# A decode attention kernel: the ring of K and V tiles aligned, dealt out by order of release, with a constant lead of K over V

## The chip, the core and the metric

The kernel runs on one core of a Trainium2 chip. TensorE (PE) multiplies matrices into PSUM and loads its weights through PEld; VectorE (DVE), ScalarE (ACT) and GpSimd (POOL) work on elements; SyncE (SP) here does nothing but issue DMA transfers, in its program's order: a transfer that has to wait for its buffer holds up every later one on SP. All engines run their own instruction lists in order and wait for one another through semaphores. 16 DMA engines move the data; a 128-partition load is shared among them, eight rows each. The metric is the device time of the program in microseconds (us), lower is better: the median of several executions.

## What is computed

One token's attention over a long cache, and a small feed-forward network beside it, mixed by a gate:

```
q = (x @ wq) as 32 heads of 128           # x: 1 x 512
scores = q . K[h] * 128**-0.5             # K: 32 heads x 65536 x 128, bf16
p = softmax(scores);  o[h] = p @ V[h]     # V like K
a = concat(o) @ wo                        # 4096 x 512
b = (silu(x @ w_gate) * (x @ w_up)) @ w_down
g = sigmoid(sum(x * gate_w));  out = g * a + (1 - g) * b
```

K and V are 512 MiB each and are read once; there is one query, so almost no arithmetic is done on each byte.

## The kernel before

**Tiles.** A head's 65536 keys lie over the partitions as 128 rows of 512 keys. CUTS = (0, 172, 344, 512) makes three tiles of each head: 172, 172 and 168 keys a partition, that is rows of 44032 or 43008 bytes, 5504 or 5376 KB a tile. There are N = 96 K tiles and 96 V tiles, n = 3h + 0, 1, 2. A ring of four slots of 44032 bytes a partition holds everything large: wq, K and V tiles, the feed-forward weights (gu_t) and at the end half of wo. The ring is a pool with four buffers used in turn: each allocation takes the slot of the allocation four earlier, and the load into it waits until that slot's last reader is done.

**Work on a K tile** (`products`, `scores`). VectorE multiplies the tile by the head's query, broadcast over the keys (L230), and folds 128 products to 16 by three halving additions (L234). TensorE sums the last 16 with an identity matrix, 16 matmuls into the head's scores in PSUM (L245). This frees the K slot.

**Softmax of a head**, once its three K tiles are scored, in the step of the next head's first K tile: `row_max` takes the maximum (L257) and spreads it over the partitions with ScalarE and a matmul (L259, L261); `exponentials` makes the probabilities (L266 to L270). VectorE does them between a first part (64 keys) of that K tile's product and the rest. `total` and `weight` sum and invert (L279 to L285).

**Work on a V tile** (`values`, L294). TensorE takes four keys of each partition at a time, 43 or 42 matmuls of 128x4 weights against 128x512, into a 4x512 accumulator. This frees the V slot. After a head's third V tile `head_copy` copies the accumulator out (ScalarE), `head_row` brings its four blocks to one row of 128 scaled by gate and softmax sum, `turn` turns four heads' rows into columns of oT with four small matmuls, and `project` multiplies them with four blocks of wo into the result a_ps. wo's first half is loaded in four pieces on the way into a pool of its own (wo_sb); its second half at the end into a ring slot (wo_t).

**Order.** It is written out by hand: `steps` (L351 to L360) is a list of pairs (n, v), and the loop from L366 emits for each step, in this order: load of V tile v, load of K tile n (both on SP); head_row of a finished head; products of K tile n on VectorE, with the softmax of the previous head within them when n starts a head; `values(v)`, then `scores(n)` on TensorE. V starts at step 3 and is therefore three tiles behind K; at steps 23, 47 and 71 (SKIPS) no V tile is taken, so that V falls four, five and six tiles behind. At step 95 two V tiles are taken, and five more steps have V alone. The last two V tiles are loaded in pieces (V_CUTS), so that TensorE can start on them early. `feed_forward_in`, `feed_forward_mid` and `feed_forward_out` lie in steps 1 and 2.

At the end (L424 to L432): copy and row of head 31, the projections of the groups that were put off (`late`), the turn of the last group, the last projection, a cast and the output.

Of the kernel before, what the change touches and what calls it, by code (L numbers as in the profile page):

```python
# [8 lines left out]
ACT = mybir.ActivationFunctionType  # L9
ALU = mybir.AluOpType  # L10
AXIS = mybir.AxisListType
P = 128
# [4 lines left out]
SLOT = 172  # L17
SLOTS = 4

WIDTH = 16  # L20

SKIPS = (23, 47, 71)


@with_exitstack
def kernel(
# [14 lines left out]
    nc = tc.nc  # L41
# [10 lines left out]
    N = H * G  # L52
# [2 lines left out]
    assert all((b - a) % 4 == 0 and b - a <= SLOT for a, b in zip(CUTS[:-1], CUTS[1:]))  # L55
    scale = float(Dh) ** -0.5

    consts = ctx.enter_context(tc.tile_pool(name="consts", bufs=1))
    ring = ctx.enter_context(tc.tile_pool(name="ring", bufs=SLOTS))
    small = ctx.enter_context(tc.tile_pool(name="small", bufs=2))  # L60
    ppool = ctx.enter_context(tc.tile_pool(name="ppool", bufs=3))
    wo_pool = ctx.enter_context(tc.tile_pool(name="wo_pool", bufs=2))
    psum_s = ctx.enter_context(tc.tile_pool(name="psum_s", bufs=2, space=bass.MemoryType.PSUM))
    psum_o = ctx.enter_context(tc.tile_pool(name="psum_o", bufs=2, space=bass.MemoryType.PSUM))
    psum_a = ctx.enter_context(tc.tile_pool(name="psum_a", bufs=1, space=bass.MemoryType.PSUM))
# [1 line left out]

    ctx.enter_context(tc.manual_schedule())

    def big(name):  # L70
        return ring.tile([P, SLOT * Dh], bf16, name=name, tag="big")


    xT = consts.tile([P, KT], bf16, name="xT")
    gwT = consts.tile([P, KT], bf16, name="gwT")
    with nc.allow_non_contiguous_dma(reason="small"):
        nc.scalar.dma_start(out=xT, in_=A_x[0, 0, :].rearrange("(p t) -> p t", t=KT))
    wq_t = big("wq_t")
    wq_sb = wq_t[:, : KT * H * Dh].rearrange("p (t f) -> p t f", t=KT)
    nc.sync.dma_start(out=wq_sb, in_=A_wq.rearrange("(p t) f -> p t f", t=KT))  # L80

# [23 lines left out]
    def span(n):  # L105
        return CUTS[n % G], CUTS[n % G + 1]

    def load(dst, cache, n, name, cuts=None):
        h = n // G
        a, b = span(n)  # L110
        t = big(name)
        view = t[:, : (b - a) * Dh].rearrange("p (j d) -> p j d", d=Dh)
        src = cache[0, h, :, :].rearrange("(p j) d -> p j d", p=P)
        cuts = cuts or (0, b - a)
        for c, d in zip(cuts[:-1], cuts[1:]):
            nc.sync.dma_start(out=view[:, c:d, :], in_=src[:, a + c : a + d, :])
        dst[n] = view
# [17 lines left out]

    for g in range(H // QG):
        queries(g)


    gu_t = big("gu_t")  # L140
    wgu_sb = gu_t[:, : 2 * KT * F].rearrange("p (w t f) -> p w t f", w=2, t=KT)
    nc.sync.dma_start(out=wgu_sb[:, 0], in_=B_w_gate.rearrange("(p t) f -> p t f", t=KT))
    nc.sync.dma_start(out=wgu_sb[:, 1], in_=B_w_up.rearrange("(p t) f -> p t f", t=KT))
# [6 lines left out]

    WH = H // 2

    def load_wo_end(cuts):
        t = big("wo_t")[:, : (H - WH) * D].rearrange("p (g t n) -> p g t n", t=WG, n=D)
        rows = A_wo[WH * P :, :].rearrange("(g p t) n -> p g t n", p=P, t=WG)
        for a, b in zip(cuts[:-1], cuts[1:]):
            nc.sync.dma_start(out=t[:, a:b], in_=rows[:, a:b])
        for g in range((H - WH) // WG):
            wo_tiles[WH // WG + g] = t[:, g]

    def load_wo(g):
        wo_tiles[g] = wo_pool.tile([P, WG, D], bf16, name="wo_sb")
# [76 lines left out]
    def scores(n):  # L239
        h = n // G  # L240
        a, b = span(n)
        if a == 0:
            S_tiles[h] = psum_s.tile([P, NBH], f32, name="S_ps")
        for c in range(WIDTH):
            nc.tensor.matmul(  # L245
                S_tiles[h][:, a:b],
                lhsT=ident_b,
                rhs=K_tiles[n][:, :, c],
                start=(c == 0),
                stop=(c == WIDTH - 1),  # L250
            )
        del K_tiles[n]

    def row_max(h):

# [31 lines left out]
    def values(n):  # L287

        h = n // G
        a, b = span(n)  # L290
        if a == 0:
            O_tiles[h] = psum_o.tile([4, 4 * Dh], f32, name="O_ps")
        for j in range(a, b, 4):
            nc.tensor.matmul(  # L294
                O_tiles[h],
                lhsT=P_tiles[h][:, j : j + 4],
                rhs=V_tiles[n][:, j - a : j - a + 4, :],
                start=(j == 0),
                stop=(j == NBH - 4),
            )  # L300
        del V_tiles[n]

    def head_copy(h, last=False):
        O_sb = small.tile([4, 4 * Dh], f32, name="O_sb")
        O_ps = O_tiles.pop(h)
        cut = 2 * Dh if last else 4 * Dh
        nc.scalar.activation(out=O_sb[:, :cut], in_=O_ps[:, :cut], func=ACT.Copy)  # L307
        if last:
            nc.vector.tensor_copy(out=O_sb[:, cut:], in_=O_ps[:, cut:])  # L309
        return O_sb  # L310

    def head_row(h, O_sb):
        oh_ps = psum_m.tile([1, P], f32, name="oh_ps", tag="misc")
        for c in range(4):
            nc.tensor.matmul(  # L315
                oh_ps,
                lhsT=ident_f[0:4, c : c + 1],
                rhs=O_sb[:, c * Dh : (c + 1) * Dh],
                start=(c == 0),
                stop=(c == 3),  # L320
            )
# [14 lines left out]
        nc.scalar.activation(out=oT[:, g * WG : (g + 1) * WG], in_=t_ps, func=ACT.Copy)  # L336
        return g

    def project(g):
        for t in range(WG):  # L340
            nc.tensor.matmul(  # L341
                a_ps,
                lhsT=oT[:, g * WG + t : g * WG + t + 1],
                rhs=wo_tiles[g][:, t, :],
                start=False,
                stop=(g == H // WG - 1 and t == WG - 1),
            )

    rows = {}

    steps = []  # L351
    v = 0
    for n in range(N):
        due = n >= G and n not in SKIPS
        steps.append((n, v if due else None))
        v += due
    v += 1
    while v < N:
        steps.append((None, v))
        v += 1  # L360

    V_CUTS = {N - 2: (0, 88, SLOT), N - 1: (0, 64, 120, 168)}

    ff = done = tot_ps = group = None
    late = []
    for n, v in steps:  # L366
        if v is not None:
            if v % (WG * G) == 2 * G and v // (WG * G) < WH // WG:
                load_wo(v // (WG * G))
            load(V_tiles, A_v_cache, v, "V_t", V_CUTS.get(v))  # L370
            if v == N - 1:
                load_wo_end((0, 1, 2, 3, 4))
        if n is not None and n > 1:
            load(K_tiles, A_k_cache, n, "K_t")
        if n == 2:
            ff = feed_forward_mid(*ff)
        if n is None:
            vector = iter(())
            size = 0
        else:  # L380
            size = span(n)[1] - span(n)[0]
            vector = products(n, 0, size)
        halves = ((0, size // 2), (size // 2, size))
        if n == 0:
            vector = (i for a, b in halves for i in products(n, a, b))
        top_of = None
        if n is None:
            top_of = H - 1 if S_tiles else None
        elif n % G == 0 and n > 0:
            top_of = n // G - 1  # L390
            vector = (i for a, b in ((0, 64), (64, size)) for i in products(n, a, b))
        if done is not None:
            head_row(done, head_copy(done))
        if top_of is not None:
            next(vector, None)
            exponentials(top_of, row_max(top_of))
        for _ in vector:
            pass
        if n == 1:
            ff = feed_forward_in()  # L400
        if n == 2:
            feed_forward_out(*ff)
        if tot_ps is not None:
            weight(*tot_ps)
            tot_ps = None
        if v is not None:
            values(v)
        if n == N - 1:
            load(V_tiles, A_v_cache, v + 1, "V_t")
            values(v + 1)  # L410
        if top_of is not None:
            tot_ps = top_of, total(top_of)
        if done is not None and done % WG == WG - 1:
            group = turn(done // WG)
        if n is not None:
            scores(n)
        if group is not None:
# [5 lines left out]
        done = v // G if v is not None and v % G == G - 1 else None  # L423
    head_row(H - 1, head_copy(H - 1, last=True))  # L424
    project(late[0])
    turn(H // WG - 1)
    for g in late[1:]:
        project(g)
    project(H // WG - 1)
# [33 lines left out]
```

## Time and profile before

| | |
|---|---|
| time, median of 3 runs | 2543.06 us (2542.61 to 2544.75) |
| profiled execution | 2544.06 us, its span 2542.3 us |
| bytes moved | 1088.54 MB, 428 GB/s over the span |
| VectorE busy | 2162.0 us (85%) |
| TensorE busy | 1652.4 us (65%) at a mean granted clock of 0.70 |
| ScalarE busy | 83.1 us (3%) |
| issue of a K load to its landing (5504 KB) | 25.2 us, median |

The profile page gives busy shares of the engines, then the span in 40 slices of 63.56 us with the DMA engines' busy share in tenths and the bytes moved; then the DMA queues; the chain of work that ended last; the groups of instructions with their mean time and what they waited for; and the DMA issues. A timeline line reads: start, length, engine, source line, operation, output <- input, shape, count, and in brackets the idle time of the engine before it with what ended that. The trace behind the page also keeps size, start and duration of each DMA packet; here a packet is one partition's row of a transfer.

### The profile page before, as it was taken

The numbers are of one execution on the slowest core, as the hardware profiler recorded it, in microseconds if no ns is written. First come the engines' busy times: TensorE is split into PE (matmuls) and PEld (weight loads), VectorE is DVE, ScalarE is ACT, GpSimd is POOL, SyncE is SP. The second block draws the span as 40 slices with busy tenths as digits, with TensorE's granted clock in tenths as the row PEclk, the third lists the DMA queues.
The fourth block names the chain that finished last, engine by engine and source line by source line (L and its number), as shares of the span: only waits on it lengthen the run. The fifth ranks groups of instructions, "written<-read, shape, count | busy, mean of one in ns | idle before, by whom it ended". The sixth has DMA issues, their size and how long they took to land.

```text
span 2542.3 us, 13985 instructions
## 1 busy us (share of the span) xinstructions
PE 1652.4 (65%) x6242; PEld 623.9 (25%) x6242; DVE 2162.0 (85%) x657; ACT 83.1 (3%) x214; POOL 0.7 (0%) x6
## 2 busy tenths in 40 slices
PE   3665666665766566766576756667657666666679
PEld 1222222222222222222122222222222222222223
DVE  6888988889988888888988888889898889888880
ACT  1000000000000000000000000000000000000000
POOL 0000000000000000000000000000000000000000
PEclk7676767666767767676667676767666767676679
DMA  9999999999999999999999999999999999999998
GB/s 416 430 435 430 432 434 429 431 434 429 414 432 434 430 433 432 429 432 433 415 427 432 434 430 431 435 429 432 435 407 431 432 433 431 433 432 430 431 434 362
DMA packets 30303, 1088.54 MB, mean 428 GB/s; under 512 B 3618, under 2 KB 3619, under 8 KB 4643
## 3 DMA queue, kind: packets, MB, share of 16 engines
q1 hardware_dynamic: 30098, 1087.65, 99.5%
q8 instruction: 49, 0.80, 0.1%
q14 instruction: 12, 0.09, 0.0%
q10 hardware_dynamic: 144, 0.00, 0.0%
HBM read 1087.64 MB, written 0.00 MB: 428 GB/s over the span
## 4 chain that ended last, share of the span: by engine, by line
DVE 44%; DMA 42%; PE 11%; issue 2%; ACT 0%; DVEq 0%; SPq 0%
DMA K_t<-in_A_k_cache_dram 41%; DVE K_t L234 22%; DVE K_t L230 21%; PE S_ps L245 9%; DMA V_t<-in_A_v_cache_dram 1%; PE O_ps L294 1%; PE mT_ps L261 1%; DMA wq_t<-in_A_wq_dram 0%; DVE m L257 0%; PE qg_ps L125 0%; ACT diag L259 0%; DVE top L266 0%; PE a_ps L341 0%; PE oh_ps L315 0%; PE a_ps L217 0%
## 5 line engine op out<-in xcount | busy, mean ns | idle before, releaser
L230 DVE TENSOR_TENSOR K_t<-K_t,q_bc 128x21504 bf16<-128x21504 bf16 (+4 forms) x128 | 1112.3, 8690 | 251.2 <-DMA K_t<-in_A_k_cache_dram 251.2
L294 PE MATMUL O_ps<-V_t,P_sb 128*4 128x512 bf16 x4096 | 1073.5, 430 | 10.4 <-ACT P_sb L270 10.0
L234 DVE TENSOR_TENSOR K_t<-K_t 128x5504 bf16<-128x5504 bf16 (+11 forms) x384 | 1016.0, 2646 | 12.2
L245 PE MATMUL S_ps<-K_t,ident_b 128*128 128x172 bf16 (+1 forms) x1536 | 458.0, 465 | 724.5 <-DVE K_t L234 724.5
L294 PEld LDWEIGHTS <-P_sb 128*4 128x4 bf16 x4096 | 374.2, 93 | 702.2 <-issue 291.6
L245 PEld LDWEIGHTS <-ident_b 128*128 128x128 bf16 x1536 | 183.5, 121 | 975.0 <-issue 812.7
L261 PE MATMUL mT_ps<-diag,ones_f 128*128 128x128 f32 x64 | 25.4, 501 | 123.4 <-ACT diag L259 123.4
L315 PE MATMUL oh_ps<-O_sb,ident_f 4*1 4x128 f32 x256 | 57.9, 399 | 1.1 <-ACT O_sb L307 1.1
L307 ACT ACTIVATE O_sb<-O_ps 4x512 f32<-4x512 f32 (+1 forms) x32 | 18.5, 579 | 1150.4 <-PE O_ps L294 1150.4
L261 PEld LDWEIGHTS mT_ps<-diag,ones_f 128*128 128x128 f32 x64 | 16.0, 311 | 141.8 <-ACT diag L259 141.8
L266 DVE TENSOR_REDUCE top<-mT_ps 128x1 f32<-128x128 f32 x32 | 9.3, 292 | 43.5 <-PE mT_ps L261 43.5
L259 ACT ACTIVATE diag<-ident_f,m 128x128 f32<-128x128 f32 x32 | 12.8, 401 | 680.8 <-DVE m L257 680.8
L315 PEld LDWEIGHTS oh_ps<-O_sb,ident_f 4*1 4x1 f32 x256 | 25.3, 108 | 35.7 <-issue 16.7
L309 DVE COPY O_sb<-O_ps 4x256 f32<-4x256 f32 x1 | 0.4, 413 | 39.2 <-ACT O_sb L307 39.2
L257 DVE TENSOR_REDUCE m<-S_ps 128x1 f32<-128x512 f32 x32 | 21.9, 685 | 7.0 <-PE S_ps L245 7.0
L325 ACT ACTIVATE o_row<-oh_ps,rg 1x128 bf16<-1x128 f32 x32 | 11.4, 358 | 423.2 <-PE oh_ps L315 423.2
L270 ACT ACTIVATE P_sb<-S_ps,bias 128x512 bf16<-128x512 f32 x32 | 22.0, 687 | 1.0
L125 PE MATMUL qg_ps<-wq_t,X_bc 128*128 128x512 bf16 x32 | 9.9, 483 | 13.2 <-DMA wq_t<-in_A_wq_dram 13.2
L284 DVE RECIPROCAL recip<-tot_ps 128x1 f32<-128x1 f32 x32 | 5.1, 160 | 11.0 <-PE tot_ps L279 11.0
L279 PEld LDWEIGHTS tot_ps<-rowsum,ones_f 128*128 128x128 f32 x64 | 9.5, 188 | 14.0 <-issue 14.0
L279 PE MATMUL tot_ps<-rowsum,ones_f 128*128 128x1 f32 x64 | 12.3, 261 | 0.0
L217 PE MATMUL a_ps<-b_sb,ones_f 1*1 1x512 f32 x2 | 1.9, 1032 | 14.3 <-ACT b_sb L216 14.3
(43 smaller groups left out, 73.2 us busy)
## 6 DMA issues: line engine op xcount, KB each, us to landing
K_t<-in_A_k_cache_dram SPq DMA_DIRECT2D x63, 5504.0 KB, 25.2
V_t<-in_A_v_cache_dram SPq DMA_DIRECT2D x63, 5504.0 KB, 24.0
K_t<-in_A_k_cache_dram SPq DMA_DIRECT2D x32, 5376.0 KB, 21.6
V_t<-in_A_v_cache_dram SPq DMA_DIRECT2D x31, 5376.0 KB, 21.4
K_t<-in_A_k_cache_dram SPq DMA_DIRECT2D x2, 2752.0 KB, 24.6
wq_t<-in_A_wq_dram SPq DMA_DIRECT2D x1, 4096.0 KB, 12.4
V_t<-in_A_v_cache_dram SPq DMA_DIRECT2D x1, 2816.0 KB, 31.6
V_t<-in_A_v_cache_dram SPq DMA_DIRECT2D x1, 2688.0 KB
```

The costliest lines, as they stand in the source:

```text
L230: yield nc.vector.tensor_tensor(out=K, in0=K, in1=q_rep, op=ALU.mult)
L234: yield nc.vector.tensor_tensor(out=K[:, :, 0:half], in0=K[:, :, 0:half], in1=K[:, :, half : 2 * half], op=ALU.add,)
L245: nc.tensor.matmul(S_tiles[h][:, a:b], lhsT=ident_b, rhs=K_tiles[n][:, :, c], start=(c == 0), stop=(c == WIDTH - 1),)
L257: nc.vector.tensor_reduce(out=m, in_=S_tiles[h], axis=AXIS.X, op=ALU.max)
L259: nc.scalar.activation(out=diag, in_=ident_f, func=ACT.Copy, scale=m)
L261: nc.tensor.matmul(mT_ps, lhsT=ones_f, rhs=diag, start=True, stop=True)
L270: nc.scalar.activation(out=P_tiles[h], in_=S_tiles[h], func=ACT.Exp, bias=bias, scale=scale, accum_out=rowsum[:, h : h + 1],)
L279: nc.tensor.matmul(tot_ps, lhsT=ones_f, rhs=rowsum[:, h : h + 1], start=True, stop=True)
L294: nc.tensor.matmul(O_tiles[h], lhsT=P_tiles[h][:, j : j + 4], rhs=V_tiles[n][:, j - a : j - a + 4, :], start=(j == 0), stop=(j == NBH - 4),)
L307: nc.scalar.activation(out=O_sb[:, :cut], in_=O_ps[:, :cut], func=ACT.Copy)
L315: nc.tensor.matmul(oh_ps, lhsT=ident_f[0:4, c : c + 1], rhs=O_sb[:, c * Dh : (c + 1) * Dh], start=(c == 0), stop=(c == 3),)
L325: nc.scalar.activation(out=rows[h // WG][:, at : at + Dh], in_=oh_ps, func=ACT.Copy, scale=rg[0:1, h : h + 1])
```

## The change

Five things are changed together.

1. A pool `edge` of 384 bytes a partition is put first, and the ring directly behind it, ahead of the small constants. The four slots thereby start at multiples of 512 bytes in a partition.
2. The ring's slots are no longer used in turn. `free` lists them; a load takes the first, and `values`, `scores` and the end of the queries and of the feed-forward network put theirs back, in the order of the program on TensorE.
3. SKIPS and the list of steps are gone. Step n has K tile n and V tile n - 4 throughout (LEAD = 4), the loads in the order K, V; four steps with V alone follow the last K tile.
4. `feed_forward_mid` is called at the end of step 1 in place of the start of step 2.
5. At the end: the last V tile has four pieces, the smallest of 20 keys, in place of three with a last one of 48. Heads 28 to 31 go to oT directly as columns (`head_column`), without row and turn; the last group of wo is loaded in the order that this needs, in rows of 1 KB. Head 31's accumulator is copied by ScalarE and VectorE into two tiles (`head_copy_two`), and the first put-off projection stands ahead of its column.

```diff
-SKIPS = (23, 47, 71)
+LEAD = 4
...
+    edge = ctx.enter_context(tc.tile_pool(name="edge", bufs=1))
+    edge.tile([P, 384], mybir.dt.uint8, name="edge")
+    ring = ctx.enter_context(tc.tile_pool(name="ring", bufs=1))
+    wo_pool = ctx.enter_context(tc.tile_pool(name="wo_pool", bufs=2))
     consts = ctx.enter_context(tc.tile_pool(name="consts", bufs=1))
-    ring = ctx.enter_context(tc.tile_pool(name="ring", bufs=SLOTS))
...
+    free = list(range(SLOTS))
+    taken = {}
     def big(name):
-        return ring.tile([P, SLOT * Dh], bf16, name=name, tag="big")
+        slot = free.pop(0)
+        t = ring.tile([P, SLOT * Dh], bf16, name=name, tag=f"big{slot}")
+        return t, slot
...
-        t = big(name)
+        t, taken[name, n] = big(name)
...
     for g in range(H // QG):
         queries(g)
+    free.append(wq_slot)
...
+            if g == H // WG - 1:
+                nc.sync.dma_start(out=wo_tiles[g], in_=rows.rearrange("(t p) n -> p t n", p=P))
+            else:
+                nc.sync.dma_start(out=wo_tiles[g], in_=rows.rearrange("(p t) n -> p t n", t=WG))
...
         del K_tiles[n]
+        free.append(taken.pop(("K_t", n)))
...
         del V_tiles[n]
+        free.append(taken.pop(("V_t", n)))
...
+    def head_copy_two(h):
         O_ps = O_tiles.pop(h)
+        low = consts.tile([4, 2 * Dh], f32, name="O_low")
+        high = consts.tile([4, 2 * Dh], f32, name="O_high")
+        nc.scalar.activation(out=low, in_=O_ps[:, : 2 * Dh], func=ACT.Copy)
+        nc.vector.tensor_copy(out=high, in_=O_ps[:, 2 * Dh :])
+        return [s[:, c * Dh : (c + 1) * Dh] for s in (low, high) for c in range(2)]
+
+    def head_column(h, O_parts):
+        oh_ps = psum_m.tile([P, 1], f32, name="oc_ps", tag="misc")
+        for c in range(4):
+            nc.tensor.matmul(
+                oh_ps, lhsT=O_parts[c], rhs=ident_f[0:4, c : c + 1], start=(c == 0), stop=(c == 3)
+            )
+        nc.scalar.activation(
+            out=oT[:, h : h + 1], in_=oh_ps, func=ACT.Copy, scale=rg[:, h : h + 1]
+        )
...
-    V_CUTS = {N - 2: (0, 88, SLOT), N - 1: (0, 64, 120, 168)}
+    V_CUTS = {N - 2: (0, 96, SLOT), N - 1: (0, 56, 108, 148, 168)}
...
-    for n, v in steps:
-        if v is not None:
+    for n in range(N + LEAD):
+        v = n - LEAD
+        if n >= N:
+            n = None
+        if n is not None and n > 1:
+            load(K_tiles, A_k_cache, n, "K_t")
+        if v >= 0:
             if v % (WG * G) == 2 * G and v // (WG * G) < WH // WG:
                 load_wo(v // (WG * G))
             load(V_tiles, A_v_cache, v, "V_t", V_CUTS.get(v))
             if v == N - 1:
-                load_wo_end((0, 1, 2, 3, 4))
-        if n is not None and n > 1:
-            load(K_tiles, A_k_cache, n, "K_t")
-        if n == 2:
-            ff = feed_forward_mid(*ff)
...
-            head_row(done, head_copy(done))
+            (head_row if done // WG < H // WG - 1 else head_column)(done, head_copy(done))
...
-        if n == N - 1:
-            load(V_tiles, A_v_cache, v + 1, "V_t")
-            values(v + 1)
...
+        if n == 1:
+            ff = feed_forward_mid(*ff)
+            free.append(gu_slot)
...
-    head_row(H - 1, head_copy(H - 1, last=True))
+    O_parts = head_copy_two(H - 1)
     project(late[0])
-    turn(H // WG - 1)
+    head_column(H - 1, O_parts)
     for g in late[1:]:
         project(g)
     project(H // WG - 1)
```

More of the change, by code (lines that the diff above doesn't have):

```diff
@@ L56 @@
     scale = float(Dh) ** -0.5
+    edge = ctx.enter_context(tc.tile_pool(name="edge", bufs=1))
+    edge.tile([P, 384], mybir.dt.uint8, name="edge")
+    ring = ctx.enter_context(tc.tile_pool(name="ring", bufs=1))
+    wo_pool = ctx.enter_context(tc.tile_pool(name="wo_pool", bufs=2))
     consts = ctx.enter_context(tc.tile_pool(name="consts", bufs=1))
-    ring = ctx.enter_context(tc.tile_pool(name="ring", bufs=SLOTS))
     small = ctx.enter_context(tc.tile_pool(name="small", bufs=2))
     ppool = ctx.enter_context(tc.tile_pool(name="ppool", bufs=3))
-    wo_pool = ctx.enter_context(tc.tile_pool(name="wo_pool", bufs=2))
     psum_s = ctx.enter_context(tc.tile_pool(name="psum_s", bufs=2, space=bass.MemoryType.PSUM))
@@ L77 @@
         nc.scalar.dma_start(out=xT, in_=A_x[0, 0, :].rearrange("(p t) -> p t", t=KT))
-    wq_t = big("wq_t")
+    wq_t, wq_slot = big("wq_t")
     wq_sb = wq_t[:, : KT * H * Dh].rearrange("p (t f) -> p t f", t=KT)
@@ L137 @@
         queries(g)
-    gu_t = big("gu_t")
+    free.append(wq_slot)
+    gu_t, gu_slot = big("gu_t")
     wgu_sb = gu_t[:, : 2 * KT * F].rearrange("p (w t f) -> p w t f", w=2, t=KT)
@@ L151, with load_wo_end @@
     WH = H // 2
[L153 to L159, printed above, removed]
+    def load_wo_end():
+        t = big("wo_t")[0]
+        for g in range(WH // WG, H // WG):
+            at = (g - WH // WG) * WG * D
+            wo_tiles[g] = t[:, at : at + WG * D].rearrange("p (t n) -> p t n", t=WG)
+            rows = A_wo[g * WG * P : (g + 1) * WG * P, :]
+            if g == H // WG - 1:
+                nc.sync.dma_start(out=wo_tiles[g], in_=rows.rearrange("(t p) n -> p t n", p=P))
+            else:
+                nc.sync.dma_start(out=wo_tiles[g], in_=rows.rearrange("(p t) n -> p t n", t=WG))
     def load_wo(g):
@@ L301, in values, with head_copy, head_row @@
         del V_tiles[n]
-    def head_copy(h, last=False):
+        free.append(taken.pop(("V_t", n)))
+    def head_copy(h):
+        O_ps = O_tiles.pop(h)
         O_sb = small.tile([4, 4 * Dh], f32, name="O_sb")
+        nc.scalar.activation(out=O_sb, in_=O_ps, func=ACT.Copy)
+        return [O_sb[:, c * Dh : (c + 1) * Dh] for c in range(4)]
+    def head_copy_two(h):
         O_ps = O_tiles.pop(h)
[L306 to L312, printed above, removed]
+        low = consts.tile([4, 2 * Dh], f32, name="O_low")
[12 more added lines that the diff above has]
+        )
+    def head_row(h, O_parts):
         oh_ps = psum_m.tile([1, P], f32, name="oh_ps", tag="misc")
@@ L317, in head_row @@
                 lhsT=ident_f[0:4, c : c + 1],
-                rhs=O_sb[:, c * Dh : (c + 1) * Dh],
+                rhs=O_parts[c],
                 start=(c == 0),
@@ L337, in turn, with project @@
         return g
-    def project(g):
-        for t in range(WG):
+    def project(g, ts=range(WG)):
+        for t in ts:
             nc.tensor.matmul(
@@ L349 @@
     rows = {}
[L351 to L360, printed above, removed]
-    V_CUTS = {N - 2: (0, 88, SLOT), N - 1: (0, 64, 120, 168)}
+    V_CUTS = {N - 2: (0, 96, SLOT), N - 1: (0, 56, 108, 148, 168)}
     ff = done = tot_ps = group = None
     late = []
-    for n, v in steps:
-        if v is not None:
+    for n in range(N + LEAD):
[5 more added lines that the diff above has]
+        if v >= 0:
             if v % (WG * G) == 2 * G and v // (WG * G) < WH // WG:
@@ L371 @@
             if v == N - 1:
-                load_wo_end((0, 1, 2, 3, 4))
-        if n is not None and n > 1:
-            load(K_tiles, A_k_cache, n, "K_t")
-        if n == 2:
-            ff = feed_forward_mid(*ff)
[L377 to L385, printed above, removed]
+                load_wo_end()
+        size = span(n)[1] - span(n)[0] if n is not None else 0
+        cuts = (0, size // 2, size) if n == 0 else (0, size)
         top_of = None
@@ L390 @@
             top_of = n // G - 1
-            vector = (i for a, b in ((0, 64), (64, size)) for i in products(n, a, b))
+            cuts = (0, 64, size)
+        vector = iter(())
+        if n is not None:
+            vector = (i for a, b in zip(cuts[:-1], cuts[1:]) for i in products(n, a, b))
         if done is not None:
-            head_row(done, head_copy(done))
+            (head_row if done // WG < H // WG - 1 else head_column)(done, head_copy(done))
         if top_of is not None:
@@ L398 @@
             pass
-        if n == 1:
-            ff = feed_forward_in()
         if n == 2:
@@ L405 @@
             tot_ps = None
-        if v is not None:
+        if v >= 0:
             values(v)
-        if n == N - 1:
-            load(V_tiles, A_v_cache, v + 1, "V_t")
-            values(v + 1)
         if top_of is not None:
@@ L414 @@
             group = turn(done // WG)
+        if n == 1:
+            ff = feed_forward_in()
         if n is not None:
             scores(n)
+        if n == 1:
+            ff = feed_forward_mid(*ff)
+            free.append(gu_slot)
         if group is not None:
@@ L422 @@
             group = None
-        done = v // G if v is not None and v % G == G - 1 else None
-    head_row(H - 1, head_copy(H - 1, last=True))
+        done = v // G if v >= 0 and v % G == G - 1 else None
+    O_parts = head_copy_two(H - 1)
     project(late[0])
-    turn(H // WG - 1)
+    head_column(H - 1, O_parts)
     for g in late[1:]:
```

## The prediction

> **What bounds the kernel now.** I read the page's strips first. The row of DMA shows the 16 engines busy to nine tenths or more in every slice; the row below gives what they moved.
>
> ```profile
> DMA  9999999999999999999999999999999999999998
> GB/s 416 430 435 430 432 434 429 431 434 429 414 432 434 430 433 432 429 432 433 415 427 432 434 430 431 435 429 432 435 407 431 432 433 431 433 432 430 431 434 362
> DMA packets 30303, 1088.54 MB, mean 428 GB/s; under 512 B 3618, under 2 KB 3619, under 8 KB 4643
> DVE 44%; DMA 42%; PE 11%; issue 2%; ACT 0%; DVEq 0%; SPq 0%
> ```
>
> A slice is 2542.3/40 = 63.56 us. The rate stands at 429 to 435 but for the first slice, slices 11, 20 and 30, and the last. The chain names VectorE and DMA in turn, because VectorE catches up and then waits for K. The bytes bind: 1088.54 MB at 432 GB/s is 2520 us of the 2542. Only some 22 us is not streaming, and the change can move that and the rate itself.
>
> Next I asked for stretches (columns: busy us of PE, PEld, DVE, ACT, POOL with counts, granted clock, DMA share, GB/s). The long ones between the dips all give 432; the dip at slice 11 holds the step without a V load (23), and slices 20 and 30 hold steps 47 and 71.
>
> ```profile
> 100.00:590.00 490.00, 322.06 (x1190) 120.33 (x1191) 423.64 (x128) 14.24 (x39) 0.00 (x0) 0.70 1.00 432
> 590.00:640.00 50.00, 24.20 (x87) 9.26 (x86) 47.90 (x14) 0.56 (x2) 0.00 (x0) 0.60 0.97 415
> 1920.00:2480.00 560.00, 375.23 (x1400) 140.52 (x1398) 481.45 (x143) 17.21 (x45) 0.00 (x0) 0.71 1.00 432
> ```
>
> The timeline around the first dip shows why: the K load at 637.42 could only go when the score matmuls from 632.69 had freed its slot. The trace's records of single packets show the engines idle 1.3 us each, their first new packet at 638.4 (1.0 us after the issue), and some 20 packets after it taking 2.0 to 2.5 us where 1.63 is usual.
>
> ```profile
> 632.69 4.71 PE L245 MATMUL S_ps<-K_t,ident_b 128*128 128x168 bf16 x16 [17.14 <-DVE K_t L234]
> 637.42 0.33 SPq L116 DMA_DIRECT2D K_t<-in_A_k_cache_dram  x1
> ```
>
> **The change part by part.** The sum is against the profiled execution, 2544.06 us (span 2542.3), 1.0 above the median of the runs shown, 2543.06.
>
> *No skipped steps.* The dips against 432: (18 + 17 + 25)/432 x 63.56 = 8.8 us. That is 1.3 to 1.6 us of idle each, and the rest slow packets. In the new order K of step n takes the slot of V(v-2), and V(v) that of K(n-2). In the steady state call K's landing T. V lands at T+13 (5504 KB at 432 GB/s is 13.05 us), its matmuls end at T+24.4 (43 x 0.26), the scores at T+29.2 (4.8). K(n+2) must start at T+39 and V(v+2) at T+52, so 14 and 23 us are to spare and no new gap follows: **-8.8**, all of it if that slack holds, 0 if each step's waits move elsewhere.
>
> *Lead of four at the start.* Here SP's queue is what to follow. New order: ..., K2, K3, K4, V0, K5, V1, K6, V2. V1 takes K3's slot, so it waits behind scores(3), and all later loads queue on SP behind it. Rows that stay:
>
> ```profile
> 66.36 11.36 DVE L230 TENSOR_TENSOR K_t<-K_t,q_bc 128x21504 bf16<-128x21504 bf16 x1 [0.48 <-DMA K_t<-in_A_k_cache_dram]
> 88.40 0.14 DVE L213 TENSOR_SCALAR rest<-gval 1x1 f32<-1x1 f32 x1
> 91.10 4.70 PE L245 MATMUL S_ps<-K_t,ident_b 128*128 128x168 bf16 x16
> 92.44 4.42 DVE L230 TENSOR_TENSOR K_t<-K_t,q_bc 128x8192 bf16<-128x8192 bf16 x1 [3.90 <-DMA K_t<-in_A_k_cache_dram]
> 96.78 0.68 DVE L257 TENSOR_REDUCE m<-S_ps 128x1 f32<-128x512 f32 x1
> 100.17 11.41 PE L294 MATMUL O_ps<-V_t,P_sb 128*4 128x512 bf16 x43 [1.43 <-ACT P_sb L270]
> 117.46 4.80 PE L245 MATMUL S_ps<-K_t,ident_b 128*128 128x172 bf16 x16 [5.55 <-DVE K_t L234]
> ```
>
> VectorE is busy from K0 on and can't go faster: K3 now waits for nothing (its 3.90 us of waiting go), but the row maximum still needs scores(2), which end at 95.80, so the maximum moves from 96.78 to 95.83, and scores(3) from 122.26 to 121.3. V1's first packet goes at 122.3. K2 leaves the engines at about 64.3 (packet records); three tiles of 13.05 and one of 12.74 later they run dry, at 116.2. Gap 6.1 us, and 1.2 us of slow packets (at the skips 2.9 lost, of it 1.3 to 1.9 idle): **+7.3**. Ends: 4.1 idle alone (if the engines run dry at 118.2, counted from VectorE's start on K2 at 66.36) and 9.0. What is late next: K6 behind values(0) (121.3 + 11.4 + 1.0 = 133.8; V1's transfer ends at 136.0, 2 to spare), V2 behind scores(4) (4 to spare), K7 (6). VectorE needs about 23.4 us a step against 26.1, so the backlog drains.
>
> *The end.* Before, five V tiles follow the last scores on TensorE; now four, but K95 comes later in the queue.
>
> ```profile
> 2454.66 20.93 PE L294 MATMUL O_ps<-V_t,P_sb 128*4 128x512 bf16 x85
> 2475.53 4.69 PE L245 MATMUL S_ps<-K_t,ident_b 128*128 128x168 bf16 x16
> 2483.47 11.02 PE L294 MATMUL O_ps<-V_t,P_sb 128*4 128x512 bf16 x43
> 2494.74 9.23 PE L294 MATMUL O_ps<-V_t,P_sb 128*4 128x512 bf16 x42
> 2505.60 25.20 PE L294 MATMUL O_ps<-V_t,P_sb 128*4 128x512 bf16 x116
> 2531.24 2.75 PE L294 MATMUL O_ps<-V_t,P_sb 128*4 128x512 bf16 x12 [0.45 <-DMA V_t<-in_A_v_cache_dram]
> 2535.43 1.02 PE L341 MATMUL a_ps<-wo_t,oT 128*1 128x512 bf16 x4
> ```
>
> With the queue's end held fixed, one tile less (V90) lies behind K95: its products start at 2453.17 + 13.05 = 2466.2 and end at 2487.9. V91 lands at 2479.3; its matmuls (43 x 0.256) end at 2490.3 and the scores, behind them, at 2495.0. The maximum (0.69 + 0.40 + 0.80 and hops) ends at 2497.1; V92 to 2507.1, copy and head to 2509.0; V93 to V95 are 128 matmuls at 25.20/116 = 0.217, 27.8 us: 2536.8. Before, values ended at 2534.0: +2.8. TensorE is late, so the finer last cut gives nothing, though every V byte is there at 2531.2. Behind it the two copies into tiles of their own lie beside project(4), and head_column spares turn and its row: 0.1 + 0.86 + 0.90 + 3.0 = 4.9 us against 5.4, -0.5. Together **+2.3** (ends: -0.3 if all V matmuls ran at 0.217, +7.3 if all at 0.256; 0.217 is what long busy rows show, so nearer the low end for the last three tiles).
>
> *Last wo group in rows of 1 KB*, four times the packets: a 4096-byte packet takes 161 ns, a 4-byte one 9, so 32 x 47 ns against 8 x 161: **+0.2**.
>
> *The ring at multiples of 512.* The built programs place it at 30944 = 60 x 512 + 224 before and at 16896 = 33 x 512 after. The trace of before has no tile load at another offset, so I bound this by the packet records. Each engine moves about 1536 rows, so one ns a row is 1.54 us. A 44032-byte row takes 1631 ns mostly, 1627 for some 70 us after each dip, at the same offset; twice the difference to a 22016-byte row (818 ns) is 1618. At most 13 ns, -20 us; at least nothing (a loss is excluded: rows and sources stay). Of the 13, 9 is what a 4-byte packet takes too, so it is no matter of place; 4 comes and goes with the state of the queue. I take a third of that: **-2.0**.
>
> [...]
>
> *Costed at nothing:* feed_forward_mid one step earlier in the text (VectorE, TensorE and ScalarE do it in the same places), pools moved, heads 28 to 30 as columns (four small matmuls under TensorE's idle time, 724.5 us before the scores).
>
> Sum: -8.8 + 7.3 + 2.3 + 0.2 - 2.0 = **-1.0**: 2543.1 for the profiled execution, **2542.1** for the median.
>
> **Rivals.**
> *A, the aligned ring quickens every row.* If 8 of the 9 ns between 1627 and 1618 belong to the crooked start, 12.3 us go in place of 2.0: 2531.8. For: the strips' bound is the stream itself. Against: a 4-byte packet costs the same 9 ns. [...]
> *B, the start doesn't drain (slower).* K6 has 2 us to spare, V2 has 4. If values(0) or scores(4) come some 4 us later than their rows, two more gaps follow, each about 2 idle and 1.2 of slow packets: +6.4, 2548.5. It decides from 2 us of lateness. For: TensorE runs at a granted clock of 0.54 to 0.76 there. Against: the rows used were taken at that clock.
> *C, no gap at the start.* If V1's transfer is not starved (scores(3) 6 us earlier), 2542.1 - 7.3 = 2534.8. Against: VectorE's rows are back to back up to there.
>
> **How the numbers follow.** 0.2% is 5.1 us, about what a measurement can tell. Forecast 0.43; A 0.27; C 0.07; B 0.23, with the cold clock at the end among its causes. So faster 0.34, same 0.43, slower 0.23. The likeliest by itself spans 2538 to 2547; the range reaches past A and B, to 2529 (A with half of C) and 2551.
>
> **What would show it.** Slices 11, 20, 30 at 430 or more; in slice 2 (430 before) a rate near 382, and SP's V load issued at about 121 behind the scores; K6 not late. Steady stretches at 432 to 433 (A: 434 to 435). The last V matmuls back to back without a wait for V, ending some 3 us later beside the last bytes. I am wrong if steady stretches change their rate, or if the second V load is out before 115.

## The result, and the profile after

The changed kernel takes **2539.04 us** (median of 13 runs, 2537.16 to 2540.97); the kernel before, run beside it, 2544.61 us (13 runs, 2542.45 to 2546.14). The ratio is 0.9979, with a 95% interval of 0.997 to 0.9987: some 5.6 us gained, at the edge of the 0.2% named in the prediction. The forecast was 2542.1 us, 3.1 us too high. The two profiled executions differ by 4.3 us: 2539.79 us (span 2538.0) against 2544.06 (span 2542.3).

The strips and the shares of the chain, kernel after (the row GB/s has 40 slices, now of 63.45 us):

```profile
GB/s 417 387 430 436 430 434 435 430 436 430 438 431 433 434 432 435 432 435 432 435 433 432 436 431 436 433 430 436 431 433 434 432 435 432 434 434 434 434 431 324
DMA packets 30830, 1088.54 MB, mean 429 GB/s; under 512 B 3633, under 2 KB 4146, under 8 KB 5170
DMA 57%; PE 22%; DVE 19%; issue 1%; ACT 0%; DVEq 0%
```

Three readings. Slices 11, 20 and 30 are no longer dips: 438, 435, 433 where 414, 415, 407 stood. Slice 2 has the new gap, 387 where 430 stood. The last slice has fallen from 362 to 324. In the chain TensorE's share has doubled, from 11% to 22%.

The stretches, kernel after (columns as before: busy us of PE, PEld, DVE, ACT, POOL, granted clock, DMA share, GB/s):

```profile
720.00:1240.00 520.00, 346.38 (x1269) 127.41 (x1269) 450.43 (x132) 15.16 (x40) 0.00 (x0) 0.71 1.00 434
1300.00:1850.00 550.00, 363.14 (x1328) 133.60 (x1328) 477.93 (x142) 16.64 (x44) 0.00 (x0) 0.71 1.00 433
1920.00:2440.00 520.00, 342.87 (x1265) 128.98 (x1265) 452.54 (x135) 16.46 (x44) 0.00 (x0) 0.72 1.00 433
```

The stream runs at 433 to 434 where it ran at 432. One GB/s of 432 is 5.9 us of the span, so this small number is the size of the whole result; the packet records resolve it better. The times of the 16128 packets of 44032 bytes:

```
kernel    mean ns   commonest times, ns (packets)
before    1635.5    1631 (8207), 1638 (3208), 1629 (1397), 1627 (1275)
after     1628.8    1627 (15963)
```

The start, kernel after (timeline):

```profile
95.71 0.33 SPq L123 DMA_DIRECT2D K_t<-in_A_k_cache_dram  x1
116.41 4.81 PE L256 MATMUL S_ps<-K_t,ident_b 128*128 128x172 bf16 x16 [16.70 <-DVE K_t L245]
121.25 0.33 SPq L123 DMA_DIRECT2D V_t<-in_A_v_cache_dram  x1
132.52 0.33 SPq L123 DMA_DIRECT2D K_t<-in_A_k_cache_dram  x1
143.40 0.33 SPq L123 DMA_DIRECT2D V_t<-in_A_v_cache_dram  x1
```

SP's V load goes at 121.25, right behind scores(3) (116.41 + 4.81). By the packet records the engines ran dry from 115.7 on and the last of them started again at 122.8; each was idle for 4.8 to 7.1 us, 6.3 in the mean. The loads at 132.52 and 143.40 come in time; no further gap follows.

The end, kernel after (timeline of TensorE):

```profile
2471.01 12.28 PE L306 MATMUL O_ps<-V_t,P_sb 128*4 128x512 bf16 x43 [9.44 <-DMA V_t<-in_A_v_cache_dram]
2483.23 4.70 PE L256 MATMUL S_ps<-K_t,ident_b 128*128 128x168 bf16 x16
2489.95 11.14 PE L306 MATMUL O_ps<-V_t,P_sb 128*4 128x512 bf16 x42
...
2502.74 27.79 PE L306 MATMUL O_ps<-V_t,P_sb 128*4 128x512 bf16 x128
2530.37 1.03 PE L369 MATMUL a_ps<-wo_t,oT 128*1 128x512 bf16 x4
...
2532.30 2.75 PE L369 MATMUL a_ps<-wo_t,oT 128*1 128x512 bf16 x12
```

The last 128 V matmuls run without a wait and end at 2530.5. The last V bytes were there at 2522.5, so at the end TensorE is what the time waits for.

**Where the 4.3 us come from.** The trace has 16 landing records for the load of a tile, read here as one for each DMA engine's part. From these records and the timelines come three numbers for every kernel of this study: when the last V piece had landed (first and last engine), when the last V matmul ended, and how late that was behind the last landing. The experiments, described below, are in it too.

| kernel | V landed, first engine | V landed, last engine | V matmuls end | late by | span |
|---|---|---|---|---|---|
| before | 2527.0 | 2531.2 | 2534.0 | 2.8 | 2542.3 |
| after | 2513.7 | 2522.5 | 2530.5 | 8.0 | 2538.0 |
| ring_at_224 | 2521.6 | 2531.4 | 2537.7 | 6.3 | 2545.2 |
| before_aligned | 2518.8 | 2523.5 | 2526.7 | 3.2 | 2535.0 |
| lead_3 | 2506.2 | 2515.3 | 2528.5 | 13.2 | 2535.9 |
| dealt_skips | 2506.5 | 2515.3 | 2517.4 | 2.1 | 2524.9 |
| ring_at_256 | 2513.6 | 2522.3 | 2528.2 | 5.9 | 2535.7 |
| ring_at_64 | 2519.9 | 2529.5 | 2536.0 | 6.5 | 2543.4 |
| skips_v_first | 2517.5 | 2522.4 | 2535.0 | 12.6 | 2542.5 |
| half_values | 2513.8 | 2519.8 | 2520.4 | 0.6 | 2528.8 |
| skips_in_turn | 2530.1 | 2533.4 | 2538.3 | 4.9 | 2545.8 |

From before to after the bytes are complete 8.7 us earlier, TensorE is 5.2 us later behind them, and what follows the last V matmul is 0.8 us shorter: -8.7 + 5.2 - 0.8 = -4.3. The experiments take these apart.

### The profile page after: what moved, and what is told of

Read it like the earlier page. It is cut to its first block, busy times and chain, and to the rows that moved or that the text cites. A ratio compares the mean times of both kernels' runs of the same rounds, so it can differ in the third digit from the quotient of the medians.

```text
span 2538.0 us, 13992 instructions
## 1 busy us (share of the span) xinstructions
PE 1672.1 (66%) x6238; PEld 625.4 (25%) x6238; DVE 2162.1 (85%) x657; ACT 82.8 (3%) x213; POOL 0.7 (0%) x6
## 4 chain that ended last, share of the span: by engine, by line
DMA 57%; PE 22%; DVE 19%; issue 1%; ACT 0%; DVEq 0%
DMA V_t<-in_A_v_cache_dram 40%; DMA K_t<-in_A_k_cache_dram 17%; PE O_ps L306 15%; DVE K_t L245 9%; DVE K_t L241 9%; PE S_ps L256 6%; PE mT_ps L273 1%; DVE m L269 0%; DMA xT<-in_A_x_dram 0%; PE qg_ps L132 0%; ACT diag L271 0%; DVE top L278 0%; PE a_ps L369 0%; PE oc_ps L333 0%; PE a_ps L228 0%
## 5 line engine op out<-in xcount | busy, mean ns | idle before, releaser
L306 PE MATMUL O_ps<-V_t,P_sb 128*4 128x512 bf16 x4096 | 1092.1, 435 | 657.7 <-DMA V_t<-in_A_v_cache_dram 657.7
L306 PEld LDWEIGHTS <-P_sb 128*4 128x4 bf16 x4096 | 384.8, 94 | 1361.0 <-issue 974.0
L256 PEld LDWEIGHTS <-ident_b 128*128 128x128 bf16 x1536 | 171.5, 116 | 356.9 <-issue 324.1
L343 PE MATMUL oh_ps<-O_sb,ident_f 4*1 4x128 f32 x224 | 52.1, 409 | 0.0
L319 ACT ACTIVATE O_sb<-O_ps 4x512 f32<-4x512 f32 x31 | 18.2, 587 | 488.2 <-PE O_ps L306 488.2
```

Of the source, the lines that this page charges most:

```text
L256: nc.tensor.matmul(S_tiles[h][:, a:b], lhsT=ident_b, rhs=K_tiles[n][:, :, c], start=(c == 0), stop=(c == WIDTH - 1),)
L306: nc.tensor.matmul(O_tiles[h], lhsT=P_tiles[h][:, j : j + 4], rhs=V_tiles[n][:, j - a : j - a + 4, :], start=(j == 0), stop=(j == NBH - 4),)
L319: nc.scalar.activation(out=O_sb, in_=O_ps, func=ACT.Copy)
L343: nc.tensor.matmul(oh_ps, lhsT=ident_f[0:4, c : c + 1], rhs=O_parts[c], start=(c == 0), stop=(c == 3),)
```

## The experiments

The experiments were timed in other sittings than the result, each with the kernel before beside it: its medians were 2544.0 to 2545.4 us there and 2544.61 beside the result, so a difference between two sittings is uncertain by about 1 us.

**The ring back at 224 above a multiple of 512, everything else as changed.**

```diff
-    edge.tile([P, 384], mybir.dt.uint8, name="edge")
+    edge.tile([P, 608], mybir.dt.uint8, name="edge")
```

> The changed kernel with its ring moved up by 224 bytes, so that it starts at 224 past a multiple of 512, as in the kernel before; all else stays. Theory P (place): a 44032-byte row takes 1631 or 1638 ns again in place of 1627, the long stretches fall from 433.25 to about 431.6 GB/s, and the time rises by 8 to 10 us, to 2547 to 2549. Theory Q (the queue: K and V now stand some 27 and 35 us in the queue, not 25, and the order of loads differs): rows stay at 1627 and the time at 2539.

Measured: 2546.96 us (2545.9 to 2547.79) beside 2544.02 for before, ratio 1.001 (1.0 to 1.0019). One stretch of it:

```profile
1300.00:1850.00 550.00, 366.15 (x1332) 134.62 (x1331) 476.22 (x141) 16.62 (x44) 0.00 (x0) 0.70 1.00 432
```

The stream is back at 432 and the rows at 1631 (8673 packets) and 1638 (3394); only 493 take 1627. So the place of the ring is worth 2546.96 - 2539.04 = 7.9 us (8.5 when each is set against the kernel before beside it), and the packets account for it: a mean of 1634.1 ns against 1628.8, 5.3 ns for each of an engine's 1536 rows, is 8.2 us. Everything else in the change together costs 2.9 us here; by the interval of the ratio that can be anything from 0 to 4.8.

**The kernel before with the ring aligned, nothing else.**

```diff
-    consts = ctx.enter_context(tc.tile_pool(name="consts", bufs=1))
+    edge = ctx.enter_context(tc.tile_pool(name="edge", bufs=1))
+    edge.tile([P, 384], mybir.dt.uint8, name="edge")
     ring = ctx.enter_context(tc.tile_pool(name="ring", bufs=SLOTS))
+    wo_pool = ctx.enter_context(tc.tile_pool(name="wo_pool", bufs=2))
+    consts = ctx.enter_context(tc.tile_pool(name="consts", bufs=1))
...
-    wo_pool = ctx.enter_context(tc.tile_pool(name="wo_pool", bufs=2))
```

> The kernel before with only its ring (and the pool of wo) put at multiples of 512; slots in turn, skipped steps and end as before. Theory P: rows take 1627 ns, the long stretches run at 433.25 GB/s, three dips stay, and the time falls by about 9 us, to 2535: faster than the changed kernel, whose new order then costs 3 to 4 us. Theory Q: rows stay at 1631, time 2543 to 2545. On the drift: the spread between the first and the last engine's landing of one tile falls back to 1 to 2 us at each dip, and stands at 4 to 5 at the end, not 9.

Measured: 2535.75 us (2533.97 to 2536.79), ratio 0.9966 (0.9953 to 0.9979). Its strip:

```profile
GB/s 417 431 436 432 435 432 431 432 436 430 411 436 433 432 435 433 433 433 432 418 429 432 436 431 432 437 432 432 436 408 433 434 433 433 435 432 432 435 431 363
```

The three dips are there (411, 418, 408), the start has none, and 15862 rows take 1627. Moving the ring alone (and with it the pools of wo and the constants) gains 8.3 us, and the kernel is 3.3 us faster than with the whole change (2.7 when each is set against the kernel before beside it). Two experiments from opposite sides thus agree: place -8, all the rest about +3.

**A lead of three in place of four.**

```diff
-LEAD = 4
+LEAD = 3
```

> The changed kernel with K three tiles ahead of V in place of four. V0 is then loaded before K4 and V1 waits for nothing late. If the gap at 115 to 122 us comes from V1's wait for scores(3), it is gone (slice 2 at 430 in place of 387, 7 us of stream). The end gets longer, since only three V tiles follow the last scores and K95 lands a tile later: 3 to 4 us. Net -3 to -4, 2535 to 2536. Rival: the gap is the price of dealing out slots; then it stays and the time is 2542 or more.

Measured: 2536.0 us (2535.08 to 2537.7), ratio 0.9968 (0.9956 to 0.9981). The strip and then the end:

```profile
GB/s 417 431 437 431 437 431 431 437 431 435 432 431 435 433 434 434 431 436 431 433 434 432 435 433 433 434 433 432 434 433 431 435 433 434 433 431 435 431 435 289
```

```profile
2488.47 4.71 PE L256 MATMUL S_ps<-K_t,ident_b 128*128 128x168 bf16 x16
...
2509.94 18.51 PE L306 MATMUL O_ps<-V_t,P_sb 128*4 128x512 bf16 x85
```

Slice 2 is at 431: no gap, and the last V byte comes 7.2 us earlier than after, which is the price of the start. But with one K tile less of lead the last scores end at 2493.2 in place of 2487.9 and three whole tiles of V wait behind them: TensorE is 13.2 us late in place of 8.0, and 5.2 of the 7.2 us go there. Neither constant lead suits both ends: three for the start, more for the end.

**Dealt slots, K ahead of V, but the skips kept: a lead of three at the start, six at the end.**

```diff
-LEAD = 4
+SKIPS = (23, 47, 71)
...
+    steps = []
+    v = 0
+    for n in range(N):
+        due = n >= G and n not in SKIPS
+        steps.append((n, v if due else -1))
+        v += due
+    while v < N:
+        steps.append((None, v))
+        v += 1
...
-    for n in range(N + LEAD):
-        v = n - LEAD
-        if n >= N:
-            n = None
+    for n, v in steps:
```

> The changed kernel (aligned ring, dealt slots, K before V, its end) with the schedule of leads of the kernel before: V starts at step 3, and steps 23, 47 and 71 take no V tile. If the dips of the kernel before came from slots used in turn (a load after a skip had to wait for the tile loaded just before), they are gone here: no slice under 428 between the first and the last two, no gap at 115 us, and six V tiles are left for the end, so that TensorE is not late there. Time about 12 us under the changed kernel, 2527. Rival: a skipped step always costs its 2.9 us, whatever the slots: then three dips stand, and the time is about 2535.

Measured: **2527.33 us** (2526.36 to 2528.04), ratio 0.9933 (0.9919 to 0.9948): the fastest of all, 16.7 us before the kernel before and 11.7 before the changed one. Strip, and end:

```profile
GB/s 419 433 432 431 438 431 432 433 432 436 431 433 433 435 433 431 433 435 434 431 433 433 433 434 433 433 433 434 434 432 434 433 433 435 431 433 434 433 436 364
```

```profile
2449.91 4.70 PE L256 MATMUL S_ps<-K_t,ident_b 128*128 128x168 bf16 x16
...
2489.59 27.79 PE L306 MATMUL O_ps<-V_t,P_sb 128*4 128x512 bf16 x128 [0.44 <-DMA V_t<-in_A_v_cache_dram]
2517.22 1.03 PE L369 MATMUL a_ps<-wo_t,oT 128*1 128x512 bf16 x4
```

No dip anywhere, skips or not; the last scores are done 33 us earlier than after, and the last 128 matmuls wait 0.44 us for their first bytes, run through, and end 2.1 us behind the last landing. So the dips of the kernel before did not need the skips to be taken away. What takes them away is told apart by the next two.

**The same, with V loaded ahead of K in each step, as before the change.**

```diff
-        if n is not None and n > 1:
-            load(K_tiles, A_k_cache, n, "K_t")
         if v >= 0:
...
             if v == N - 1:
                 load_wo_end()
+        if n is not None and n > 1:
+            load(K_tiles, A_k_cache, n, "K_t")
```

> The kernel of the dealt slots with skipped steps, but each step loads V before K again. With two loads a step in that order the list deals out the same slots as using them in turn does. If the dips of the kernel before come from that pairing (after a skip a load waits for the scores of the tile loaded last but one), three dips come back in slices 11, 20 and 30 and the time is near 2538 to 2540. If dealing by itself removed them, none is seen and the time stays at 2527.

Measured: 2544.3 us, one run (before beside it 2545.38). Strip and end:

```profile
GB/s 416 440 431 436 428 438 429 432 435 425 420 433 432 434 434 433 433 434 432 420 434 430 437 429 438 430 436 432 435 414 430 433 436 432 434 433 434 431 435 299
```

```profile
2466.88 4.71 PE L256 MATMUL S_ps<-K_t,ident_b 128*128 128x168 bf16 x16 [10.42 <-DVE K_t L245]
...
2507.22 27.79 PE L306 MATMUL O_ps<-V_t,P_sb 128*4 128x512 bf16 x128
```

The dips are back (420, 420, 414), and bytes are complete 7.1 us later. The time is 4 to 6 us above what that theory expected: K95 comes a tile later here, so that its scores end at 2471.6 (2454.6 in the version before), and TensorE is 12.6 us late, which that expectation did not count. This is one run.

**The same as the fastest, K first, but the slots used in turn.**

```diff
+    turn_of = list(range(SLOTS))
...
-        slot = free.pop(0)
+        slot = turn_of.pop(0)
+        turn_of.append(slot)
```

> The version with three skipped V tiles and K loaded ahead of V (2527.33 us with dealt slots), its four slots now used strictly in turn. Theory 1, the order of the loads alone removes the dips: 2526 to 2529 us, slices 11, 20 and 30 at 430 or more. Theory 2, the dealing is needed as well: behind a skip, K of step n+3 falls to the slot of K of step n+1, whose scores end some 51 us after the landing of K of step n, when the engines run dry at 52 and the first packet follows the issue by 1 us; three dips of about 1 us idle and 1.2 us of slow packets, 2532 to 2535 us, and the engines' spread at the end smaller than 8.8 us.

Measured: 2546.46 us (2544.5 to 2547.67), ratio 1.0008 (0.9999 to 1.0018): 19.1 us slower than with dealt slots, more than the second theory's 5 to 8. Strip, and the timeline at the first dip:

```profile
GB/s 416 388 438 431 432 438 430 431 433 437 403 429 438 429 435 432 435 432 432 403 429 438 427 438 430 438 430 437 430 407 434 430 438 429 436 431 437 430 435 360
```

```profile
634.14 11.95 PE L308 MATMUL O_ps<-V_t,P_sb 128*4 128x512 bf16 x42
...
652.93 4.82 PE L258 MATMUL S_ps<-K_t,ident_b 128*128 128x172 bf16 x16 [6.52 <-DVE K_t L247]
...
657.77 0.33 SPq L125 DMA_DIRECT2D K_t<-in_A_k_cache_dram  x1
658.20 0.38 SPq L125 DMA_DIRECT2D V_t<-in_A_v_cache_dram  x1
```

Against it the same place with dealt slots:

```profile
627.39 11.10 PE L306 MATMUL O_ps<-V_t,P_sb 128*4 128x512 bf16 x42
638.52 0.33 SPq L123 DMA_DIRECT2D K_t<-in_A_k_cache_dram  x1
646.18 4.82 PE L256 MATMUL S_ps<-K_t,ident_b 128*128 128x172 bf16 x16 [7.37 <-DVE K_t L245]
651.02 0.33 SPq L123 DMA_DIRECT2D V_t<-in_A_v_cache_dram  x1
```

Dealt, the K load takes the slot that the V matmuls have just left, at 638.5; in turn, it must wait for the scores (652.93 + 4.82), though the V matmuls had ended at 646.1, and the V load behind it goes out at the same moment. By the packet records the engines are then idle for 4.0, 4.2 and 3.5 us at the three places, and for 5.9 at the start, where K5 falls to the slot of K3 and waits for its scores until 120.9: 17.6 us of idle, and the last V byte comes 18.1 us later. The second theory had the place right and the price of each gap too small, and it had left out the start. So neither the order of the loads nor the dealing removes the dips alone; the two together do.

**The ring at 256 above a multiple of 512, and at 64.** Two kernels; the first has an edge of 640 bytes, the second of 448.

```diff
-    edge.tile([P, 384], mybir.dt.uint8, name="edge")
+    edge.tile([P, 640], mybir.dt.uint8, name="edge")
```

> The changed kernel with its ring at 256 past a multiple of 512. [...] If 512 is the unit that counts, as the words of the change have it, rows take 1631 and 1638 ns again, 432 GB/s, and the time is near 2547.

> The changed kernel with its ring at 64 past a multiple of 512. If 64 bytes is the unit that counts, rows take 1627 ns (433 GB/s); if it is 256 or 512, 1631 and 1638 (432 GB/s, time near 2547).

Measured, one run each: 2537.44 and 2545.21 us. One stretch of the ring at 256:

```profile
1300.00:1850.00 550.00, 360.85 (x1328) 133.34 (x1328) 478.01 (x142) 16.64 (x44) 0.00 (x0) 0.71 1.00 433
```

and of the ring at 64:

```profile
1300.00:1850.00 550.00, 360.72 (x1328) 133.51 (x1328) 476.58 (x141) 16.62 (x44) 0.00 (x0) 0.71 1.00 432
```

At 256 the rows take 1627 (15948 packets; mean 1628.9), as at 512. At 64 they take 1629 (7854) and 1636 (3133), mean 1632.6. So of the four places tried the two at multiples of 256 give the short rows; 64 above one costs 3.9 ns a row, 224 above one 5.3. No place between 64 and 224 was tried, so the runs do not settle which unit counts.

**Half of the V matmuls left out**, to see whether the end is TensorE's.

```diff
-        for j in range(a, b, 4):
+        for j in range(a, b, 8):
...
-                stop=(j == NBH - 4),
+                stop=(j == NBH - 8),
```

> The changed kernel with every second matmul of V left out (all bytes are still loaded; the output is then not the attention's). About a third of TensorE's instructions go. Theory D (drift): the engines drift apart because each 16 KB of instructions fetched takes one of them some 0.9 us of time; 49 fetches fall to about 33, and the spread between first and last landing of a late tile from 8.9 to about 6 us. Rival: the spread comes from the loads themselves and stays at 9. Theory T (the end is bound by TensorE): values end within 1.5 us of the last V landing in place of 8 us after it, so the time falls by 8 us and some 2 more for the spread, to about 2529; if the end were bound by the bytes it would not fall by more than the spread's 2 to 3.

Measured: 2530.62 us, one run, 8.4 below the changed kernel's median. Queue of instruction fetches, kernel after and then this one (packets, MB, share of the engines' time):

```profile
q8 instruction: 49, 0.80, 0.1%
q8 instruction: 33, 0.54, 0.1%
```

And the last V matmuls of this one:

```profile
2518.24 1.24 PE L306 MATMUL O_ps<-V_t,P_sb 128*4 128x512 bf16 x5 [1.37 <-DMA V_t<-in_A_v_cache_dram]
2519.82 0.59 PE L306 MATMUL O_ps<-V_t,P_sb 128*4 128x512 bf16 x2 [0.34 <-DMA V_t<-in_A_v_cache_dram]
```

TensorE now waits for each piece of the last tile and is done 0.6 us behind the last landing. The end of the changed kernel was bound by TensorE, for 7 to 8 us.

## Why the prediction came out near, point by point

**The gap at the start: right.** It was worked out as idle from 116.2 to 122.3, 6.1 us, and 7.3 with slow packets. Measured: 6.3 us of idle, 0.6 of slow packets, and 7.2 us between the last landings with a lead of four and of three. Rival C is out.

**The backlog drains: right.** No load of the following steps is late, and by the packet records the stream has no further gap before its end. Rival B is out.

**The dips, -8.8: the mechanism right, the sum not whole.** The slices rose to 438, 435 and 433. But with the ring at the old place the last V byte came at 2531.4, against 2531.2 before; -8.8 + 7.3 had promised 1.5 us earlier. The term was counted in the mean rate of 16 engines, while the end waits for the last of them. The table's first two columns show it: before, the engines finish 4.2 us apart, with the ring at 224 and the new order 9.8. The first engine did gain, 5.4 us. In a dip the engines that are behind have work left while the others idle: in the first dip of before, by the packet records, three of the 16 engines do not idle at all and the others for 0.4 to 3.2 us. So a dip costs the last engine less than the mean, and its removal gives the last engine less. More on this below.

**The end, +2.3: right in kind, too small.** The forecast had the V matmuls end 5.6 us behind the last landing (2536.8 against 2531.2); it was 8.0 here, 5.9 to 6.5 in the three kernels that differ in the ring's place alone. The 27.79 us for the last 128 matmuls is the 27.8 of the working. What the working had too short were the 43 and 42 matmuls before them, 12.28 and 11.14 us where rows of before gave 11.0 and 10.0: together 2.4 us, as much as the difference. They follow a wait of 9.44 us, and the granted clock from 2470 to 2502 is 0.79; before, it was 0.83 to 0.87 between 2440 and 2505. The ring at 256 ran them in 10.89 and 10.44, though behind a wait of 9.18 us, so the wait alone does not settle how long they take; what sets the clock there, no run shows. The upper end of the term (+7.3) covers it. The chain behind the matmuls gave -0.8 for -0.5.

**The ring's place, -2.0: the step that failed.** It is -7.2 in the spans (2545.2 to 2538.0), -7.9 in the medians. The prediction's own sign says so too: it was to be wrong if the steady stretches changed their rate, and with the ring's place they went from 432 to 433 and 434, between the 432 to 433 of the forecast and the 434 to 435 of rival A. That the stream bounds the kernel and that a nanosecond a row is 1.54 us was right, and so was that rows do not go below 1627 to speak of (in the kernel after none of the 16128 took under 1625): the 9 ns between 1627 and 1618 stayed, as did the 9 ns of a 4-byte packet. What failed is the size of "a third of 4 ns". The 1627 seen behind dips was put down to the state of the queue and largely written off, when it was the time that nearly every aligned row takes; and the difference was read from the commonest time, 1631, when a fifth of the rows took 1638. With the mean in place of the commonest time the same working would have started from 1635.5 - 1627 = 8.5 ns, 13 us, with the slow packets behind the dips in it; the place alone is 5.3 ns. Why a misplaced row takes 1631 and, for one in five, 1638, and why it comes down to 1627 behind a gap, stays open.

Rival A was therefore the better account of the stream in kind: the aligned ring quickens every row, by 5.3 ns where it had 8. Its working was off, for it looked for the gain below 1627 ns, where the rows did not go, and its 2531.8 us is further from the measured 2539.04 than the forecast is. No run shows its 8 ns of a row: the runs show 5.3 for 224 above a multiple of 512, 3.9 for 64, and as good as nothing for 256 (mean 1628.9 against 1628.8). In all of them the address written was moved, and the one read stayed.

**The sum.** Order and end cost 2.9 us (ring at 224 against before) where +1.0 was worked out; the place gave 7.9 where 2.0 was. The two errors have opposite signs, so the forecast is nearer than its parts: that it came within 3.1 us is in part luck.

## What to carry to other kernels

Where a stream of large DMA packets bounds the time, look at the mean time of a packet and at the address it is written to: moving the ring from 224 above a multiple of 512 to a multiple was worth 7.9 and 8.3 us of 2544 in the two experiments on it, more than the whole change, whose other parts cost 3. The gaps in this stream were a question of which buffer the next load waited for (17.6 us of idle with the slots used in turn): let it take the buffer that came free first and queue the loads in that order, and the lead of one stream over the other can then be chosen for each end by itself (three at the start, six at the end: 2527.33 us). And count a gain in the stream on the engine that ends last, then ask who is late behind it.

## What the runs showed that was not expected

**The DMA engines drift apart.** The spread between the first and the last engine's landing of one tile grows between gaps, to 8.9 us in the kernel after, and falls at them: in the kernel before from 3.5 to 1.7, from 3.7 to 1.0 and from 4.6 to 1.2 us at its three dips. From the landing records, spread in us at about the same times:

```
us            103   602   1003  1508  1920  2436
before        1.8   3.5   2.3   3.0   1.8   3.9
after         1.7   3.1   4.5   5.9   7.4   8.9
half_values   1.9   1.8   2.9   4.5   4.5   5.8
```

After rises in steps of about 1.4 us, one every 415 to 430 us; before falls back behind each dip. The profile page counts 49 transfers in the queue of instruction fetches over the run, each of 16 KB and some 0.93 us on one engine, about one in 52 us. As far as start and end of the packets let one follow an engine, they go to 8 of the 16 engines in turn, so that a round takes some 415 us. With half of the V matmuls left out there are 33 of them, and the spread ends at 5.8 to 5.9 in place of 8.9: 33/49 of 8.9 is 6.0. A step is more than the 0.93 us of one fetch, and the packet records show the rest: the data row that follows a fetch on the same engine takes 0.49 us more than its usual 1627 ns (median over the fetches of the kernel after), and 0.93 + 0.49 is 1.42 us. With half of the matmuls left out a round of 8 fetches takes some 615 us, and the spread goes from 1.7 to 3.0, 4.4 and 5.8 us, near 810, 1430 and 2070 us. So size and pace of the steps fit the fetches in both kernels; no run took the fetches away altogether.
